# Whole-row query weights for layers 0 and 1, stored head columns for layers 2 and 3, and another order of steps at the layer ends

## The chip, the cores and the metric

The kernel runs on one core of one Trainium2 chip. The metric is the device time of one execution in microseconds (us). The kernel before took 2003.76 us (median of three runs, 2003.35 to 2005.01). A profiled execution gives a span (first to last instruction) shorter than the time of the same execution: 2002.9 us in the profile of before.

In the profiles PE is TensorE (matmuls; PEld are its weight loads), DVE is VectorE, ACT is ScalarE, POOL is GpSimd, and SP is SyncE, which issues the loads. The granted clock is the share of TensorE's full clock that the profile records at a time.

## The reference

Four attention layers decode one token. Layers 0 and 2 use the tensors A, layers 1 and 3 the tensors B. Each layer has its own pass over the whole cache:

```python
D, H, Sk, Dh = 640, 32, 8192, 192          # bfloat16
def _A_ref(x, k_cache, v_cache, wq, wo):   # _B_ref is the same
    q = (x @ wq).reshape(...)              # 1 x 32 heads x 192
    scores = einsum("bhqd,bhkd->bhqk", q, k_cache) * Dh ** -0.5
    p = softmax(scores)
    o = einsum("bhqk,bhkd->bhqd", p, v_cache)
    return o.reshape(...) @ wo
for l in range(4):                         # A, B, A, B
    x = x + ref(layernorm(x), ...)
```

K and V of one head are 3072 KB each; 32 heads, two tensors and four layers give most of the 849 MB that the profile counts. The query weights wq are 640 x 6144, 7680 KB.

## The kernel before

The kernel keeps eight slots in SBUF, of 128 x 12288 bfloat16, one K or V tile each. One queue issues all loads in the order of `plan`; a load waits until the tile that held its slot has been used. The engines work through `steps`: "m" (products: DVE multiplies K by q in place, in four pieces, and PE sums the products into S with 24 matmuls), "s" (softmax), "v" (values: 32 matmuls on PE), "wq" (query columns from a part of wq), "wc" and "wo" (output projection). The output weights of the last two heads, "wol", are a separate small load.

```python
HEADS_W, Q_FIRST, O_LAST, NSLOT = 10, 2, 2, 8
KEPT = {0: {("k", 0), ("v", 0)}, 1: {("v", 28), ("v", 29), ("v", 30), ("v", 31)}}
Q_PARTS = [(c, min(2, DC - c)) for c in range(0, DC, 2)]      # DC = 5: 2 + 2 + 1 chunks of rows
# ... cut ...
steps, plan = [], []
for l in range(NL):
    if l == 0:
        plan.append(("k", 0, 0))
        plan.append(("wq0", 0))
    wq_early = l == 2
    if wq_early:
        plan += [("wq", l, g) for g in range(len(Q_PARTS))]
    for p in range(H):
        if p > 0 and p % HEADS_W == 0:
            b = p // HEADS_W - 1
            steps.append(("wc", l, b))
            if p <= H - HEADS_W:
                plan.append(("wo", l, b))
                steps.append(("wo", l, b))
        if first_load("k", l, p) == ("k", l, p) and (l, p) != (0, 0):
            plan.append(("k", l, p))
        if stays("k", l, p):
            plan.append(("t", l, p))
        if wq_early and p == 0:
            part = [("wq", l, 0), ("m", l, 0), ("wq", l, 1), ("s", l, 0), ("v", l, 0), ("wq", l, 2)]
        elif p < H - 2:
            part = [("m", l, p), ("s", l, p), ("v", l, p)]
        elif p == H - 2:
            part = [("m", l, p)]
        else:
            part = [("m", l, p), ("s", l, p - 1), ("s", l, p), ("v", l, p - 1), ("v", l, p)]
        steps += part
        plan += [n for n in part if n[0] == "v" and first_load(*n) == n]
        if not wq_early:
            for g in {0: [0], 1: [1, 2]}.get(p, []):
                plan.append(("wq", l, g))
                steps.append(("wq", l, g))
        if p == H // 2 + 4 and l + 1 < NL:
            plan.append(("wq0", l + 1))
    plan.append(("wo", l, 2))
    steps.append(("wo", l, 2))
    plan.append(("wol", l))
at = {n: i for i, n in enumerate(steps)}

# ... cut ...
```

`KEPT` tiles stay in SBUF for the layer two further on: K and V of head 0 from layer 0 to layer 2, V of heads 28 to 31 from layer 1 to layer 3. So at the end of layer 1 six of the eight slots hold kept tiles and two rotate. The columns of wq for the first two heads, `wq0`, are a load of their own in every layer, because a layer can begin when these have landed:

```python
if n[0] == "wq0":
    return SP.op(lambda s: s.dma_start(
        wq0[:], w["wq"][:, o["q0"]:o["q0"] + Q_FIRST * DH].rearrange("(p c) n -> p c n", c=DC)),
        freed.get(("wq0", l - 1)), sem=semQ0, inc=16)
if n[0] == "wol":
    wol = slot[place[("wo", l, 2)]][:, NW * D:(NW + OI) * D].rearrange("p (i n) -> p i n", n=D)
    return SP.op(lambda s: s.dma_start(
        wol, w["wo"][o["wol"] * DH:(o["wol"] + O_LAST) * DH].rearrange("(p i) n -> p i n", p=P)),
        sem=semOL, inc=16)
```

The eviction of the value sums to SBUF, one instruction a head:

```python
ev_os[h] = last["O"][par] = last["rl"][par] = AC.op(
    lambda a: a.activation(o_sb[:], OB[par][:, 0:2 * DH], ACT.Copy, scale=rl[par][:, 0:1]),
    e, ev_rl[h], last["osb"], bank=use[f"O{par}"])

```

## Time and profile before

| | before |
|---|---|
| time, median of three | 2003.76 us |
| span of the profiled execution | 2002.9 us |
| PE, DVE, ACT busy | 70%, 52%, 11% |
| share of DMA in the chain of waits | 70% |
| a 3072 KB transfer lands every | 7.30 us |
| last K landing to final addition (the tail) | 25.8 us |

These are lines of the profile page of before. The first two rows have a digit or number for each of 40 equal slices of 50 us: the busy share of the DMA engines in tenths, and what they moved. The last is the chain of work that ended last.

```profile
DMA  9999999999999999999999999999999999999997
GB/s 404 433 430 426 431 430 426 431 431 428 425 431 429 431 429 430 426 432 428 429 375 432 430 429 431 431 427 430 429 429 428 430 428 431 431 429 429 429 431 321
...
DMA packets 44055, 850.65 MB, mean 425 GB/s; under 512 B 4800, under 2 KB 7360, under 8 KB 7872
...
HBM read 849.35 MB, written 0.00 MB: 424 GB/s over the span
...
DMA 70%; PE 17%; DVE 12%; ACT 1%; issue 1%; another core or an unknown queue 0%; SPq 0%; DVEq 0%
```

Nearly every slice is at about 430 GB/s, so the queue's time is the kernel's time. Three slices fall short: the start (404), the slice at 1000 to 1050 us (375) and the end (321). The slice at 1000 us holds the end of layer 1. Here is that end in the timeline of before. The columns are start, duration, engine, line, operation, out<-in, shapes, count, and in brackets the idle time before it and what ended it.

```profile
992.65 6.76 DVE L433 TENSOR_TENSOR slot<-slot,q_sb 128x3072 bf16<-128x3072 bf16 x4 [2.19 <-DMA slot<-in_B_k_cache_dram]
...
999.96 6.76 DVE L433 TENSOR_TENSOR slot<-slot,q_sb 128x3072 bf16<-128x3072 bf16 x4 [0.54 <-DMA slot<-in_B_k_cache_dram]
1006.64 0.68 DVE L453 TENSOR_REDUCE s_sb<-S 128x64 f32<-128x512 f32 x1
1006.77 1.46 PE L58 MATMUL S<-slot,ident 128*128 128x512 bf16 x6 [0.21 <-DVE slot L433]
...
1018.24 0.58 ACT L490 ACTIVATE o_sb<-O,small 128x384 f32<-128x384 f32 x1 [1.25 <-PE O L482]
...
1020.31 3.16 PE L402 MATMUL YB<-oT,slot 128*128 128x1 bf16 x75 [0.22 <-DMA slot<-in_B_wo_dram]
...
1024.10 0.38 SPq L272 DMA_DIRECT2D slot<-in_A_wq_dram  x1
1024.11 0.16 DVE L559 TENSOR_TENSOR small<-small,YB 128x5 f32<-128x5 f32 x1 [11.67 <-PE YB L402]
...
1038.75 0.34 SPq L269 DMA_DIRECT2D slot<-in_A_k_cache_dram  x1
```

**L** is the landing of head 30's K, the last but one of layer 1 (992.63 us in before, just ahead of the first line). The products of heads 30 and 31 follow each other at once, 7.3 us apart, as their K tiles land. **z** is the addition that closes the layer (1024.11, or L+31.5). At about the same time the queue, whose fastest part had nothing left from 1020.28 on (the slowest landed its last data at 1028.33), gets its next load, the second part of layer 2's wq. **Next K** is the first K that layer 2 loads; it is issued at 1038.75 (L+46.1) and lands at 1049.96 (L+57.3).

By the slowest of a transfer's 16 parts, next K landed 10.7 us after its predecessor instead of 7.3: this is the stall of 3.4 us that the prediction speaks of.

A landing here is always that of the slowest of a transfer's 16 parts. The Trainium skill, "DMA: Bandwidth & Descriptors", Why a DMA increments its semaphore by 16, says that only the full 16 means that all data landed. The landing records agree that it matters: the first and last part of head 30's K landed 8.1 us apart (984.52 and 992.63), and compute began 0.02 us after the last.

### The profile page before, as it was taken

The numbers are of one execution on the slowest core, as the hardware profiler recorded it, in microseconds if no ns is written. First come the engines' busy times: TensorE is split into PE (matmuls) and PEld (weight loads), VectorE is DVE, ScalarE is ACT, GpSimd is POOL, SyncE is SP. The second block draws the span as 40 slices with busy tenths as digits, with TensorE's granted clock in tenths as the row PEclk, the third lists the DMA queues.
The fourth block names the chain that finished last, engine by engine and source line by source line (L and its number), as shares of the span: only waits on it lengthen the run. The fifth ranks groups of instructions, "written<-read, shape, count | busy, mean of one in ns | idle before, by whom it ended". The sixth has DMA issues, their size and how long they took to land.

```text
span 2002.9 us, 20412 instructions
## 1 busy us (share of the span) xinstructions
PE 1406.5 (70%) x10438; PEld 323.9 (16%) x7494; DVE 1047.1 (52%) x1072; ACT 217.6 (11%) x657; POOL 4.6 (0%) x22
## 2 busy tenths in 40 slices
PE   5666767667667767767777676676677768767667
PEld 1111111111211111111131111111112212111112
DVE  3454554556345456455535546545564465554554
ACT  0111111111011111111101111111110111111110
POOL 0000000000000000000000000000000000000000
PEclk8788888888688798787878888888886888887887
DMA  9999999999999999999999999999999999999997
GB/s 404 433 430 426 431 430 426 431 431 428 425 431 429 431 429 430 426 432 428 429 375 432 430 429 431 431 427 430 429 429 428 430 428 431 431 429 429 429 431 321
DMA packets 44055, 850.65 MB, mean 425 GB/s; under 512 B 4800, under 2 KB 7360, under 8 KB 7872
## 3 DMA queue, kind: packets, MB, share of 16 engines
q1 hardware_dynamic: 43824, 849.37, 99.3%
q8 instruction: 70, 1.15, 0.2%
q14 instruction: 17, 0.14, 0.0%
q10 hardware_dynamic: 144, 0.00, 0.0%
HBM read 849.35 MB, written 0.00 MB: 424 GB/s over the span
## 4 chain that ended last, share of the span: by engine, by line
DMA 70%; PE 17%; DVE 12%; ACT 1%; issue 1%; another core or an unknown queue 0%; SPq 0%; DVEq 0%
DMA slot<-in_A_k_cache_dram 35%; DMA slot<-in_B_k_cache_dram 34%; PE S L58 11%; DVE slot L433 10%; PE O L482 2%; DMA slot<-in_A_wq_dram 1%; PE S L446 1%; PE TB L497 1%; DVE s_sb L453 1%; ACT p_sb L463 1%; PE TB L467 0%; PE QT L366 0%; DVE small L460 0%; PE YB L402 0%
## 5 line engine op out<-in xcount | busy, mean ns | idle before, releaser
L433 DVE TENSOR_TENSOR slot<-slot,q_sb 128x3072 bf16<-128x3072 bf16 x512 | 865.8, 1753 | 465.3 <-DMA slot<-in_A_k_cache_dram 239.5
L58 PE MATMUL S<-slot,ident 128*128 128x512 bf16 x2944 | 795.6, 424 | 34.1 <-DVE slot L433 34.1
L482 PE MATMUL O<-slot,p_sb 128*2 128x384 bf16 x4096 | 356.8, 428 | 0.0
L446 PE MATMUL S<-slot,ident 128*128 128x512 bf16 x128 | 60.9, 476 | 249.4 <-DVE slot L433 249.2
L453 DVE TENSOR_REDUCE s_sb<-S 128x64 f32<-128x512 f32 x128 | 88.4, 691 | 241.6 <-PE S L58 241.6
L482 PEld LDWEIGHTS O<-slot,p_sb 128*2 128x2 bf16 x4096 | 130.5, 88 | 138.9 <-issue 106.5
L497 PE MATMUL TB<-o_sb,small 128*1 128x192 f32 x480 | 124.0, 391 | 36.3 <-DVE small L471 28.0
L392 ACT ACTIVATE q_sb<-QM 128x192 bf16<-128x192 f32 x120 | 39.7, 331 | 970.7 <-PE QM L385 970.7
L385 PEld LDWEIGHTS QM<-ident,qT 128*128 128x128 bf16 x240 | 23.0, 98 | 731.2 <-issue 715.9
L467 PE MATMUL TB<-small,ones 128*128 128x1 f32 x256 | 50.7, 267 | 109.9 <-ACT p_sb L463 109.9
L457 PE MATMUL QM<-ident,m_bf 128*128 128x128 bf16 x128 | 27.7, 216 | 129.5 <-DVE m_bf L456 129.5
L490 ACT ACTIVATE o_sb<-O,small 128x384 f32<-128x384 f32 x128 | 74.4, 581 | 238.8 <-PE O L482 238.8
L471 DVE RECIPROCAL small<-TB 128x1 f32<-128x1 f32 x128 | 21.5, 168 | 123.3 <-PE TB L467 123.3
L463 ACT ACTIVATE p_sb<-s_sb,small 128x64 bf16<-128x64 f32 x128 | 44.5, 348 | 290.7 <-DVE small L460 290.7
L446 PEld LDWEIGHTS S<-slot,ident 128*128 128x128 bf16 x128 | 12.7, 99 | 331.3 <-DVE slot L433 330.9
L460 DVE TENSOR_REDUCE small<-QM 128x1 f32<-128x128 f32 x128 | 37.3, 291 | 53.2 <-PE QM L457 53.2
L467 PEld LDWEIGHTS TB<-small,ones 128*128 128x128 f32 x256 | 39.9, 196 | 129.6 <-ACT p_sb L463 129.6
L503 ACT ACTIVATE orow<-TB 1x192 bf16<-1x192 f32 x120 | 38.4, 320 | 205.4 <-PE TB L497 205.4
L497 PEld LDWEIGHTS TB<-o_sb,small 128*1 128x1 f32 x480 | 33.5, 89 | 77.7 <-DVE small L471 37.2
L457 PEld LDWEIGHTS QM<-ident,m_bf 128*128 128x128 bf16 x128 | 12.2, 96 | 208.1 <-ACT q_sb L392 131.6
L402 PE MATMUL YB<-oT,slot 128*128 128x1 bf16 x900 | 37.9, 178 | 3.1 <-ACT oT L417 2.2
L402 PEld LDWEIGHTS YB<-oT,slot 128*128 128x128 bf16 x900 | 36.9, 131 | 3.9 <-ACT oT L417 2.9
(47 smaller groups left out, 220.3 us busy)
## 6 DMA issues: line engine op xcount, KB each, us to landing
slot<-in_B_k_cache_dram SPq DMA_DIRECT2D x64, 3072.0 KB, 36.1
slot<-in_A_k_cache_dram SPq DMA_DIRECT2D x63, 3072.0 KB, 23.2
slot<-in_A_v_cache_dram SPq DMA_DIRECT2D x63, 3072.0 KB, 26.3
slot<-in_B_v_cache_dram SPq DMA_DIRECT2D x60, 3072.0 KB, 36.9
slot<-in_A_wo_dram SPq DMA_DIRECT2D x6, 2400.0 KB, 26.3
slot<-in_B_wo_dram SPq DMA_DIRECT2D x6, 2400.0 KB, 34.0
slot<-in_A_wq_dram SPq DMA_DIRECT2D x4, 2880.0 KB, 22.2
slot<-in_B_wq_dram SPq DMA_DIRECT2D x4, 2880.0 KB, 30.7
```

Source lines behind the costliest of these rows:

```text
L58: return t.add_instruction(mybir.InstMatmult(name=t.bass.get_next_instruction_name(), engine=mybir.EngineType.PE, ins=[t.lower_ap(rhs), t. ...
L392: lambda a: a.activation(q_sb[i][:], QM[:, 0:DH], ACT.Copy), e, last["q"][i], bank=use["QM"])
L402: e = PE.op(lambda t, i=i, c=c, f=y_first[0], fin=fin: t.matmul(YB[:, c:c + 1], lhsT=t3[:, i, c:D:DC], rhs=o[:, i:i + 1], start=f, stop=fi ...
L433: e = DV.op(lambda v, d0=d0: v.tensor_tensor(k3[:, :, d0:d0 + QD], kin[:, :, d0:d0 + QD], q_sb[qi][:, d0:d0 + QD].unsqueeze(1).broadcast_t ...
L446: t.matmul(S[:, :], lhsT=ident[:], rhs=k3[:, :, d0:d0 + R], start=True, stop=fin) if d0 == 0 else
L453: ev_s = DV.op(lambda v: v.tensor_reduce(s_sb[par][:], S[:].rearrange("p (j r) -> p j r", r=R), AX.X, ALU.add), ev_S[h], last["s"][par], b ...
L457: e = PE.op(lambda t: t.matmul(QM[:, C_MX:C_MX + P], lhsT=m_bf[par][:, 0:1].broadcast_to([P, P]), rhs=ident[:], start=True, stop=True), ev ...
L463: ev_p[h] = AC.op(lambda a: a.activation(p_sb[par][:], s_sb[par][:], ACT.Exp, bias=negm[par][:, 0:1], accum_out=l_col[par][:]), ev_n, ev_s ...
L467: e = PE.op(lambda t: t.matmul(TB[:, C_L + par:C_L + par + 1], lhsT=ones[:], rhs=l_col[par][:], start=True, stop=True), ev_p[h], last["L"] ...
L482: e = PE.op(lambda e, g=g, j=j, f=m < G, fin=fin: e.matmul(OB[par][32 * g:32 * g + 2, 0:2 * DH], lhsT=p_sb[par][:, j:j + 2], rhs=t[:, j * ...
L490: lambda a: a.activation(o_sb[:], OB[par][:, 0:2 * DH], ACT.Copy, scale=rl[par][:, 0:1]),
L497: e = PE.op(lambda t, i=i: t.matmul(TB[0:1, C_O:C_O + DH], lhsT=pick[:, i:i + 1], rhs=o_sb[:, i * DH:(i + 1) * DH], start=(i == 0), stop=( ...
```

## The change

The intent is to take small packets out of the queue and to shorten the chain at the layer ends.

1. Layers 0 and 1 load wq as one transfer of whole rows, 61,440 B each, over three neighbouring slots. The slots become one tensor `pool`.
2. While that wq is in SBUF, DVE copies the first two heads' columns for the layer two further on. Layers 2 and 3 load no `wq0`.
3. The last two heads of a layer get another order: the softmax of head 30 before the products of head 31, and its values before the softmax of head 31.
4. Other edits at layer ends: layers 2 and 3 take wq as 1 + 2 + 2 chunks instead of 2 + 2 + 1. The small output weights lie beside the next layer's wq part instead of beside the large ones, so the slot of the large ones is free after the first projection. The last layer's large output weights are split. The value sums of the last two heads are evicted in two pieces. Layer 3's first wq part comes before its first K, and the constant `ones` shrinks to one column that is broadcast.

```diff
+    Q_PARTS = [[(0, 2), (2, 2), (4, 1)] if l < 2 else [(0, 1), (1, 2), (3, 2)] for l in range(NL)]
+        pool = sb("pool", [P, NSLOT * TS], BF16)
+        slot = [pool[:, i * TS:(i + 1) * TS] for i in range(NSLOT)]
+        wq0 = [sb(f"wq0{i}", [P, DC, Q_FIRST * DH], BF16) for i in range(2)]
 ... cut ...
-                    part = [("m", l, p), ("s", l, p - 1), ("s", l, p), ("v", l, p - 1), ("v", l, p)]
+                    part = [("s", l, p - 1), ("m", l, p), ("v", l, p - 1), ("s", l, p), ("v", l, p)]
-                if p == H // 2 + 4 and l + 1 < NL:
-                    plan.append(("wq0", l + 1))
 ... cut: placement of three neighbouring slots, of the small output weights, the split of the last load ...
+            elif n[0] == "wq" and l < 2:
+                f = lambda s: s.dma_start(pool[:, i * TS:i * TS + DC * QW], w["wq"].rearrange("(p c) n -> p (c n)", c=DC))
 ... cut ...
+                q0 = ORDER[l + 2]["q0"]
+                ev_first[l] = DV.op(lambda v: v.tensor_copy(wq0[l][:], whole[:, :, q0:q0 + Q_FIRST * DH]), e)
 ... cut ...
-                ev_os[h] = last["O"][par] = last["rl"][par] = AC.op(
-                    lambda a: a.activation(o_sb[:], OB[par][:, 0:2 * DH], ACT.Copy, scale=rl[par][:, 0:1]),
+                if h < H - O_LAST:
+                    parts = [(o_sb[:], OB[par][:, 0:2 * DH])]
+                else:
+                    q = 1 if O_PART[l] == P else O_PART[l] // O_LAST // 8
+                    parts = [(o_sb[:, i * DH:(i + 1) * DH].rearrange("p (i e q) -> p q e i", i=OI[l], q=q),
+                              OB[par][:, i * DH:(i + 1) * DH].rearrange("p (q e i) -> p q e i", i=OI[l], q=q))
+                             for i in range(2)]
```

## The prediction

> **What bounds it now.** The DMA queue. The slices show DMA 9/10 busy and 425-433 GB/s, except the first (404), the one at 1000-1050 us (375, end of layer 1) and the last (321). The chain of waits is 70% DMA (K transfers). A 3072 KB transfer lands every 7.30 us; PE (70%) and DVE (52%) wait for data. So three things pay: queue time, queue stalls, and the tail after the last K.
>
> The landing records show each transfer's 16 parts spreading: first and last are 8.1 us apart at 1010 us, 2.0 after the stall there, 8.3 at the end. The slowest part releases compute; I count on it.
>
> **Queue time removed.** The four 480 KB loads of the first heads' columns cost 1.40-1.46 us each in landing spacing (2.1 in start-up): 2560 packets of 768 B, 36 ns each, while 19,200 B take 718 ns and 24,576 B 915 ns. The line through those two leaves 14 ns fixed per packet; the Trainium skill ("DMA: Bandwidth & Descriptors", Why small descriptors are slow) tells of a fixed cost per packet; this trace agrees. After: layers 2 and 3 load none (-1.46 us each). Layers 0 and 1 load 61,440 B rows: estimated 8 x 2.27 = 18.1 us against 40 x 0.435 + 1.46 = 18.9 now, -0.7 each. Splitting the last output-weight load: +0.06. Together -4.3 us, all on the critical path.
>
> **End of layer 1.** Six slots hold kept tiles, two rotate. Now the slowest part waits about 3.4 us (next K lands 10.7 us after its predecessor, not 7.3): the second wq part is issued at 1024.1, when both output projections are done, the first K of layer 2 at 1038.8, after 90 query matmuls (2.6 us) that delay its slot. After: the second wq part waits for the first projection only, and 45 matmuls come first. But softmax of head 30 (2.8 us of DVE in line) now precedes head 31's products, so the layer ends about 2 us later. Stall 3.4 -> 2.2: -1.2 us.
>
> **Other boundaries.** Layer 1's whole wq needs three free slots, but some 20 us of V and wo are queued behind the last K when they come free (8-12 us after landing): no stall. First products move from 17.0 to about 28 us; initial transfers last to about 50, slots are free by about 35: no cost. The column copy (1-2 us DVE) is off the path.
>
> **Tail.** From the last K landing (1973.9) to the final add (1999.7) the chain is DVE/PE, not DMA (last weights land 1995.4). Products 31 start about 3.1 us later; against that, values 30 no longer stand behind softmax 31 (-2.9). Output projection: 90 matmuls before and after. Net 0, +-1.
>
> **Prediction.** 2003.8 - 4.3 - 1.2 = 1998.2 us, range 1993.5 to 2001.5. Faster by over 2%: 0.01; within: 0.98; slower: 0.01.
>
> **What would show it.** HBM read 848.37 MB, no 768 B packets; whole wq landing about 18 us after its predecessor; slice at 1000-1050 at 380-395 GB/s; first K of layer 2 landing about 3 us earlier; softmax between products 30 and 31 on DVE; last slice about unchanged.
>
> **What would make it wrong.** 61,440 B rows moving at another rate; a DMA gap at layer 0/1; the slowest part drifting otherwise (its lag grows in steps near 0.6-1.3 us, probably instruction fetches of 16 KB): +-1.5; another PE clock in the tail (0.5 now); the layer-1 gap closing fully (-2) or growing.

## More of the kernel before

The Trainium skill, "Perfetto Trace Analysis", Optimization Strategy, says that a kernel sometimes has several regimes, with a most-contended engine that changes over time. This trace agrees: the queue, at about 430 GB/s, sets the time in nearly all slices, and the chain from L to next K in this one (375 GB/s).

The windows view of before shows the same place in stretches of 5 us. Its columns are the stretch, its length, the busy time and count of PE, PEld, DVE, ACT and POOL, then the granted TensorE clock, the DMA share and GB/s.

```profile
1000.00:1005.00 5.00, 4.89 (x22) 0.10 (x1) 5.00 (x4) 0.00 (x0) 0.00 (x0) 1.00 0.97 413
1005.00:1010.00 5.00, 3.32 (x15) 0.40 (x3) 3.21 (x7) 0.44 (x2) 0.00 (x0) 1.00 1.01 434
...
1020.00:1025.00 5.00, 4.26 (x93) 4.09 (x93) 0.43 (x5) 0.17 (x1) 0.00 (x0) 0.74 0.62 259
...
1035.00:1040.00 5.00, 5.00 (x73) 1.54 (x59) 0.91 (x2) 0.00 (x0) 0.00 (x0) 0.89 0.79 280
```

PE is busy and at full clock while the last scores are summed, and the queue falls to 259 GB/s only from 1020 us on. It is short again from 1035 to 1040 us (280 GB/s), until next K is issued.

## The result, and the profile after

The changed kernel took 2004.01 us (median of four runs, 2001.93 to 2005.47); before took 2003.55 us in its four runs. Ratios here are from the runs of both kernels in the same rounds, so they are not quite the ratio of the quoted medians or means. The ratio is 1.0002, with a 95% interval from 0.9984 to 1.0019. The predicted gain of 5.5 us did not come. The spans of the two profiled executions differ by 1.3 us (2001.53 against 2002.86), which lies inside the interval.

Lines of the page of after:

```profile
DMA  9999999999999999999989999999999999999997
GB/s 412 430 430 431 430 429 428 432 430 430 429 428 431 430 429 430 430 430 430 429 351 431 430 429 429 431 431 429 429 430 427 428 430 430 431 429 431 428 431 319
...
DMA packets 40487, 849.67 MB, mean 425 GB/s; under 512 B 4688, under 2 KB 4688, under 8 KB 5328
...
HBM read 848.36 MB, written 0.00 MB: 424 GB/s over the span
...
DMA 66%; PE 20%; DVE 11%; ACT 1%; issue 1%; another core or an unknown queue 0%; SPq 0%; DVEq 0%
```

The 2560 packets of 768 B and 0.99 MB are gone, as intended. But the slice at 1000 us fell from 375 to 351 GB/s, where 380 to 395 was predicted, and DMA's share of the chain fell from 70% to 66% in favour of PE. Here is the same place in the timeline of after:

```profile
989.84 6.76 DVE L492 TENSOR_TENSOR pool<-pool,q_sb 128x3072 bf16<-128x3072 bf16 x4 [1.97 <-DMA pool<-in_B_k_cache_dram]
...
999.90 0.69 DVE L512 TENSOR_REDUCE s_sb<-S 128x64 f32<-128x512 f32 x1 [3.30 <-PE S L58]
...
1002.56 6.75 DVE L492 TENSOR_TENSOR pool<-pool,q_sb 128x3072 bf16<-128x3072 bf16 x4
1004.76 7.63 PE L58 MATMUL S<-pool,ident 128*128 128x512 bf16 x23
...
1019.12 0.94 ACT L556 ACTIVATE o_sb<-O,small 128x192 f32<-128x192 f32 x2 [2.38 <-PE O L541]
...
1021.49 3.16 PE L462 MATMUL YB<-oT,pool 128*128 128x1 bf16 x75
...
1024.68 0.38 SPq L324 DMA_DIRECT2D pool<-in_A_wq_dram  x1
...
1025.28 0.16 DVE L630 TENSOR_TENSOR small<-small,YB 128x5 f32<-128x5 f32 x1 [9.66 <-PE YB L462]
...
1037.68 0.34 SPq L319 DMA_DIRECT2D pool<-in_A_k_cache_dram  x1
```

L is 989.82, so all that came before it gained 2.8 us. Then DVE, which had been done with head 30's products at 996.60, stood idle for 3.30 us until PE had summed their scores. Only then came the softmax, and only after it head 31's products: at L+12.7, where before had them at L+7.3. z came at L+35.5 instead of L+31.5, and next K landed at 1049.58, L+59.8 instead of L+57.3. Of the 2.8 us, 2.4 had been given back.

The windows of after, in the same columns as above:

```profile
1000.00:1005.00 5.00, 1.23 (x5) 0.50 (x4) 3.63 (x6) 0.44 (x2) 0.00 (x0) 0.80 1.00 427
1005.00:1010.00 5.00, 5.00 (x13) 0.00 (x0) 4.31 (x3) 0.00 (x0) 0.00 (x0) 0.52 0.94 403
1015.00:1020.00 5.00, 3.78 (x46) 2.03 (x46) 0.17 (x1) 1.05 (x3) 0.00 (x0) 0.66 0.81 336
1020.00:1025.00 5.00, 4.88 (x100) 4.87 (x101) 0.00 (x0) 0.23 (x2) 0.00 (x0) 0.50 0.06 22
...
1035.00:1040.00 5.00, 4.96 (x104) 2.42 (x91) 1.83 (x4) 0.00 (x0) 0.00 (x0) 1.00 1.03 436
```

PE had little to do from 1000 to 1005 us (1.23 us of 5, before 4.89), because it waited for products that waited for the softmax. In the next stretch its clock was 0.52, and 13 score matmuls filled 5.00 us, where before did 12 and three small ones in 3.32 us at clock 1.00. The queue moved almost nothing (22 GB/s) from 1020 to 1025 us. The stall had changed its place. By the slowest of a transfer's 16 parts, the second wq load landed 12.8 us after the first (7.1 in before, for 6.9 us of data), next K only 7.6 us after its predecessor. The first wq load is 1440 KB here instead of 2880 KB, so the queue had less to do while the layer ended.

The part from L to next K in pieces, from the two traces (us; each figure is rounded by itself):

| piece | before | after | difference |
|---|---|---|---|
| L to start of head 31's products | 7.3 | 12.7 | +5.4 |
| to end of head 31's score matmuls | 8.3 | 9.8 | +1.6 |
| to z | 15.9 | 12.9 | -3.0 |
| z to issue of next K | 14.6 | 12.4 | -2.2 |
| issue to landing of next K | 11.2 | 11.9 | +0.7 |
| sum, L to next K | 57.3 | 59.8 | +2.4 |

From next K to the last K of layer 3 after gained another 1.6 us, mostly the wq0 of layer 3 that is not loaded (1.40 us in before). The last K landed at 1971.95 against 1973.90. The tail from there to the final addition was 26.0 us against 25.8.

### The profile page after: what moved, and what is told of

It reads as the page before. It is cut to its first block, busy times and chain, and to the rows that moved or that the text cites. A ratio compares the mean times of both kernels' runs of the same rounds, so it can differ in the third digit from the quotient of the medians. Undisturbed runs are those within 1.5% of the kernel's fastest.

```text
span 2001.5 us, 20412 instructions
## 1 busy us (share of the span) xinstructions
PE 1399.3 (70%) x10438; PEld 321.3 (16%) x7494; DVE 1049.4 (52%) x1074; ACT 219.8 (11%) x665; POOL 4.5 (0%) x22
## 4 chain that ended last, share of the span: by engine, by line
DMA 66%; PE 20%; DVE 11%; ACT 1%; issue 1%; another core or an unknown queue 0%; SPq 0%; DVEq 0%
DMA pool<-in_A_k_cache_dram 32%; DMA pool<-in_B_k_cache_dram 31%; PE S L58 13%; DVE pool L492 10%; PE O L541 2%; DMA pool<-in_B_wq_dram 1%; DMA x_bf<-in_A_x_dram 1%; PE TB L564 1%; PE S L505 1%; DVE s_sb L512 1%; PE QT L424 1%; PE YB L462 1%; ACT p_sb L522 1%; PE TB L526 0%
## 5 line engine op out<-in xcount | busy, mean ns | idle before, releaser
L492 DVE TENSOR_TENSOR pool<-pool,q_sb 128x3072 bf16<-128x3072 bf16 x512 | 865.6, 1753 | 431.5 <-DMA pool<-in_A_k_cache_dram 221.5
L58 PE MATMUL S<-pool,ident 128*128 128x512 bf16 x2944 | 795.5, 424 | 35.8 <-DVE pool L492 35.7
L541 PE MATMUL O<-pool,p_sb 128*2 128x384 bf16 x4096 | 354.0, 426 | 0.0
L505 PE MATMUL S<-pool,ident 128*128 128x512 bf16 x128 | 60.1, 469 | 231.3 <-DVE pool L492 231.3
L541 PEld LDWEIGHTS O<-pool,p_sb 128*2 128x2 bf16 x4096 | 130.0, 88 | 169.5 <-issue 137.0
L556 ACT ACTIVATE o_sb<-O,small 128x384 f32<-128x384 f32 (+1 forms) x136 | 77.3, 580 | 273.9 <-PE O L541 273.9
L505 PEld LDWEIGHTS S<-pool,ident 128*128 128x128 bf16 x128 | 12.7, 99 | 289.9 <-DVE pool L492 289.8
L462 PE MATMUL YB<-oT,pool 128*128 128x1 bf16 x900 | 38.0, 178 | 2.2 <-ACT oT L476 2.2
L462 PEld LDWEIGHTS YB<-oT,pool 128*128 128x128 bf16 x900 | 37.0, 131 | 2.9 <-ACT oT L476 2.9
## 6 DMA issues: line engine op xcount, KB each, us to landing
pool<-in_B_k_cache_dram SPq DMA_DIRECT2D x64, 3072.0 KB, 35.5
pool<-in_A_wo_dram SPq DMA_DIRECT2D x6, 2400.0 KB, 26.8
```

What stands on the lines that cost most here:

```text
L58: return t.add_instruction(mybir.InstMatmult(name=t.bass.get_next_instruction_name(), engine=mybir.EngineType.PE, ins=[t.lower_ap(rhs), t. ...
L462: e = PE.op(lambda t, i=i, c=c, f=y_first[0], fin=end and i == k - 1: t.matmul(YB[:, c:c + 1], lhsT=t3[:, i, c:D:DC], rhs=o[:, i:i + 1], s ...
L492: e = DV.op(lambda v, d0=d0: v.tensor_tensor(k3[:, :, d0:d0 + QD], kin[:, :, d0:d0 + QD], q_sb[qi][:, d0:d0 + QD].unsqueeze(1).broadcast_t ...
L505: t.matmul(S[:, :], lhsT=ident[:], rhs=k3[:, :, d0:d0 + R], start=True, stop=fin) if d0 == 0 else
L541: e = PE.op(lambda e, g=g, j=j, f=m < G, fin=fin: e.matmul(OB[par][32 * g:32 * g + 2, 0:2 * DH], lhsT=p_sb[par][:, j:j + 2], rhs=t[:, j * ...
L556: ev_os[h] = AC.op(lambda a, o=o, i=i: a.activation(o, i, ACT.Copy, scale=rl[par][:, 0:1]), e, ev_rl[h], last["osb"], bank=use[f"O{par}"])
```

## The experiments

The first theory (T1) was that the order of the last two heads costs what the queue gained. The rivals were that the queue's gain is smaller than estimated, that the two-piece eviction or the placement of the small weights costs it, and that the restart of the queue after layer 1 is decided by when the second wq part is issued and not by the compute chain. All kernels gave correct results. They ran in four sets, each with its own nine runs of before. Times are medians of five runs; times of one set differ by chip from another's, so ratios are what to compare.

### The order alone, in both kernels

`a_oldorder` is after with one line put back; `b_neworder` is before with that line put in.

```diff
 (a_oldorder; b_neworder has the reverse edit in the kernel before)
-                    part = [("s", l, p - 1), ("m", l, p), ("v", l, p - 1), ("s", l, p), ("v", l, p)]
+                    part = [("m", l, p), ("s", l, p - 1), ("s", l, p), ("v", l, p - 1), ("v", l, p)]
```

> The changed kernel with one thing undone: at layer ends the order of the last two heads is that of before (products 31, then softmax 30, softmax 31, values 30, values 31). I call T the landing (slowest part) of the last K of layer 1. Measured from T to the landing of the next K loaded (second head of layer 2): 50.0 us before, 52.4 after. Theory (order): the new order makes layer 1 end about 4 us later (T+24.2 before, T+28.1 after), the second wq part waits for that layer's output projection, so the queue runs dry. With the old order the layer ends near T+24, the second wq part is issued near T+23.4, and T to next K is 47 to 48 us, so the kernel is 4 to 5 us shorter than the changed one, near 1998 us, 5 to 6 us below before. Rival (the smaller first wq part, 1440 instead of 2880 KB, leaves too little in the queue, and the order costs nothing): T to next K stays 51 us or more and the time within 1.5 us of the changed kernel.

> The kernel before with one thing done: the new order of the last two heads alone. Theory (order costs): layer 1 ends near T+28, T to next K grows from 50.0 to about 53 us, the tail stays within 1 us, so the kernel is about 3 us slower than before (2006 to 2007 us). Rival (order costs nothing, the queue part sizes do): T to next K stays within 0.7 us of 50.0, and the time equals that of before within 1 us.

Measured: a_oldorder 2000.93 us, ratio 0.9985 [0.9973, 0.9998]; b_neworder 2006.13 us, ratio 1.0008 [0.9995, 1.0020]. With the old order head 31's scores ended at L+15.6 again, and with the new order in the kernel before at L+21.1. Both times moved in the direction of T1, but neither is clear of noise by itself: b_neworder's interval holds 1, and a_oldorder's overlaps after's. a_oldorder's time missed the expected 1998 us, and the marks that the expectations named missed too. From the last K of layer 1 to next K it took 51.7 us in a_oldorder (47 to 48 expected, the rival's mark was 51 or more) and 50.0 us in b_neworder (about 53 expected, the rival's mark was 50.0). In b_neworder that last K itself landed 1.7 us late (L+9.0), and from L, which later expectations use, next K moved from L+57.3 to L+59.0. In a_oldorder z was still at L+33.9 (before L+31.5) and next K at L+59.0, hardly earlier than in after. So the order isn't the only cost at the end of layer 1: in this trace both sets of value matmuls ran at half clock (2.73 us each; 2.73 and 1.47 in before), and the two-piece eviction was still there.

### Filling the queue earlier

`c_wo_early` is after with layer 1's large output weights ahead of the last V, and projected before the last values. That frees their slot, and so the second wq part of layer 2, earlier. `d_wo_early_tail` does the same at the last layer too.

```diff
+EARLY = (1,)                        # d_wo_early_tail: (1, 3)
 ... cut ...
+                if l in EARLY and p == H - 1:
+                    part = part[:-1] + [("wo", l, 2)] + part[-1:]
                 steps += part
-                plan += [n for n in part if n[0] == "v" and first_load(*n) == n]
+                plan += [n for n in part if n[0] == "wo" or n[0] == "v" and first_load(*n) == n]
 ... cut: no second "wo" after the last head; the last values are gathered before the small projection ...
```

> The changed kernel with the last large output weight of layer 1 loaded ahead of the last V instead of behind it, and multiplied ahead of the last values, so that its slot is free for the second wq part about 8 us sooner; the new order stays. Theory (the gap is made by the second wq part waiting for the layer's end): the second wq part is issued near T+17 instead of T+27.5, no gap in the queue before it, T to next K 46.5 to 48 us, about 5 us less than the changed kernel, about 1998 us. Rival (the gap is bandwidth or start-up of transfers after the layer end, whatever the issue): T to next K stays above 50.5 us.

> The one before it in this list, with the same done at the end of layer 3: there the first 12 columns of the last large output weight come ahead of the last V and are multiplied ahead of the last values, the 3 other columns while ScalarE evicts the last values, and the small output part last. Boundary as in the one before. Tail: from the landing of the last K of layer 3 to the final addition 26.0 us in the changed kernel (25.8 before); expected 24.7 us, so 1.3 us less in all, about 1996.5 us. If the tail was bound by the last V's landing instead, it would grow by about 3 us, since that V now lands 4.6 us later.

Measured: c_wo_early 2004.23 us, ratio 0.9997 [0.9984, 1.0009]; d_wo_early_tail 2002.89 us, ratio 0.9997 [0.9983, 1.0010]. The second wq part was issued at L+28.4 instead of L+34.9, with hardly a gap for the slowest part before it (it landed 7.3 us after the first), and still next K landed at L+59.1, against L+59.8 in after. The gap had only moved: the third part was issued at L+39.1, and next K's slot comes free with head 0's products, which stand behind z (L+34.5), so next K was issued at L+48.2. In after itself the loads behind the second part landed one right after another, so there its issue did set the landing of next K; but the gate that stands behind it is less than 1 us away. This is against the rival, and against the prediction, which had booked a gain for an earlier second part. The expected times (about 1998 and 1996.5 us) were both missed. The tail of d_wo_early_tail (24.9 us) is no shorter than that of c_wo_early (24.6), whose tail is unchanged; no gain is shown there.

`e_k_slot` attacks the new gate: c_wo_early, with the query columns of the second wq part computed before head 0's products, so that next K can take that part's slot.

```diff
-                steps.append(("wq", l, 0))
+                steps += [("wq", l, 0), ("wq", l, 1)]
-                    part = [("m", l, 0), ("wq", l, 1), ("s", l, 0), ("v", l, 0), ("wq", l, 2)]
+                    part = [("m", l, 0), ("s", l, 0), ("v", l, 0), ("wq", l, 2)]
```

> The kernel with the output weight ahead of the last V of layer 1, plus one thing: the second wq part's query columns run on PE ahead of head 0's product matmuls, so that the next K takes that wq part's slot and not the slot of head 0's K. Theory (what gates the restart is the slot that head 0's products free, at the end of a DVE/PE chain from L, not the wq parts): the next K is issued at about L+42.5 instead of L+48.2 and lands at L+55.5 to L+57, against L+59.1 in the kernel without this; 2 to 3 us less in time than that kernel. Rival (the restart is gated by wq parts or by bandwidth): next K still lands at L+58.5 or later.

Measured: 2002.91 us, ratio 0.9991 [0.9979, 1.0004]. Next K was issued at L+43.0, five us earlier, and landed at L+58.9 all the same, which is what its rival had forecast. In the plan it stands behind the third wq part, which was issued only at L+40.6 and landed at L+50.2, because its slot waits for the first part's query columns, behind z. Its tail was 26.8 us, with the same code there as c_wo_early (24.6): the tail alone varies by 2 us from trace to trace.

### The parts of the change

`g_wq_only` keeps points 1 and 2 of the change and undoes 3 and 4. `f_one_evict` is after with the one-piece eviction.

```diff
 (g_wq_only against after, core)
-    Q_PARTS = [[(0, 2), (2, 2), (4, 1)] if l < 2 else [(0, 1), (1, 2), (3, 2)] for l in range(NL)]
+    Q_PARTS = [[(0, 2), (2, 2), (4, 1)] for l in range(NL)]
-                    part = [("s", l, p - 1), ("m", l, p), ("v", l, p - 1), ("s", l, p), ("v", l, p)]
+                    part = [("m", l, p), ("s", l, p - 1), ("s", l, p), ("v", l, p - 1), ("v", l, p)]
-            if n[0] == "wol" and n[1] + 1 < NL:  ...
+            if n[0] == "wol":
                 before[n] = []               # the small output weights lie beside the large ones
 (both, against after)
-                for o, i in parts:
-                    ev_os[h] = AC.op(lambda a, o=o, i=i: a.activation(o, i, ACT.Copy, scale=rl[par][:, 0:1]),
+                ev_os[h] = AC.op(lambda a: a.activation(o_sb[:], OB[par][:, 0:2 * DH], ACT.Copy, scale=rl[par][:, 0:1]),
```

> The first part of the change alone: whole rows of wq in layers 0 and 1, the first heads' columns copied for layers 2 and 3; everything at layer ends as before (order of the last two heads, one-piece eviction, small output part behind the large one in its slot, two-column first wq parts, no split at the end). I call L the landing of the next-to-last K of layer 1. Before: next K of layer 2 is issued at L+46.1 and lands at L+57.3; the changed kernel L+47.9 and L+59.8. Theory (whole rows gain what was predicted, the layer-end edits of the change lose it at the end of layer 1): L is about 2.8 us earlier than in before, the next K lands at L+57 to L+57.8, the last K of layer 3 lands 4 to 4.5 us earlier than before, and the kernel is 3.5 to 4.5 us faster than before, 2 us or more faster than the changed kernel. Rival (the saved queue time itself does not survive the end of layer 1, whatever the order there): next K at L+59 or later, gain at most 2 us.

> The changed kernel with the last two heads' results evicted in one piece of 384 (as before, 0.58 us) instead of two strided pieces (0.94 us together), the gather reading with a stride again. If the two pieces are part of what makes layers end later, layer 1 ends 0.7 us sooner than in the changed kernel (L+34.8 instead of L+35.5), and the tail is 0.7 us shorter; if they are hidden, nothing moves. In time at most 1.5 us below the changed kernel, not clear of noise.

Measured: g_wq_only 2000.17 us (1999.31 to 2000.71), ratio 0.9978 [0.9965, 0.9992]; f_one_evict 2002.95 us, ratio 0.9995 [0.9983, 1.0008]. g_wq_only is 4.4 us faster than before (means 2000.10 and 2004.48), and its last K landed at 1969.23 us, 4.67 earlier than before's: the predicted queue time was there. In f_one_evict z was at L+34.9, as expected if the eviction counts, but next K at L+60.0: the eviction alone doesn't explain the end of layer 1.

The page's GB/s row of g_wq_only:

```profile
GB/s 411 429 431 430 428 430 431 430 429 429 431 428 430 431 429 429 430 431 429 430 383 430 428 431 431 429 430 429 430 430 427 430 429 430 431 428 431 430 431 314
```

The slice at 1000 us is at 383, inside the 380 to 395 that had been predicted for after. The timeline of g_wq_only there:

```profile
997.21 6.76 DVE L484 TENSOR_TENSOR pool<-pool,q_sb 128x3072 bf16<-128x3072 bf16 x4 [0.54 <-DMA pool<-in_B_k_cache_dram]
1003.89 0.69 DVE L504 TENSOR_REDUCE s_sb<-S 128x64 f32<-128x512 f32 x1
...
1021.43 0.16 DVE L612 TENSOR_TENSOR small<-small,YB 128x5 f32<-128x5 f32 x1 [11.44 <-PE YB L451]
...
1035.20 0.34 SPq L308 DMA_DIRECT2D pool<-in_A_k_cache_dram  x1
```

Head 31's products start at L+7.3 with a wait of 0.54 us for their K, not for a softmax, and next K is issued at 1035.20, landing at 1046.76 (L+56.9; 2.8 us earlier than after). Its windows show the clock:

```profile
1000.00:1005.00 5.00, 5.00 (x25) 0.10 (x1) 4.80 (x5) 0.00 (x0) 0.00 (x0) 1.00 1.00 428
1005.00:1010.00 5.00, 2.00 (x18) 0.98 (x18) 1.73 (x6) 0.88 (x4) 0.00 (x0) 1.00 0.99 423
```

### After again

The unchanged kernel after, in the same set as e, f and g, to see how far two traces of one kernel differ.

> The changed kernel unaltered, to compare in the same rounds and to have a second trace: next K of layer 2 lands at L+59.8 within 1 us, layer 1 ends at L+35.5 within 1 us, and the time is within 1.5 us of before. If the clock granted to PE at the end of layer 1 varies from run to run, the layer's end moves by up to 1.3 us per set of 32 value matmuls (1.5 or 2.7 us each).

Measured: 2003.63 us, ratio 0.9998 [0.9985, 1.0010]. z was at L+34.6 (below f_one_evict's, without its edit) and next K at L+58.8, about 1 us less than in the first trace, so +1.5 us against before instead of +2.4. A difference of 1 us between two traces' marks is therefore not evidence by itself.

### The remaining parts, one at a time

`i_parts` is a_oldorder with the one-piece eviction: g_wq_only plus the placement edits. `g_neworder` is g_wq_only with the order line of after. `h_wo_early_old` is i_parts with the early output weights of c_wo_early. `j_order_l1` is g_wq_only with the order at layer 1 only.

```diff
 (i_parts against a_oldorder: the eviction edit shown above)
 (g_neworder against g_wq_only)
-                    part = [("m", l, p), ("s", l, p - 1), ("s", l, p), ("v", l, p - 1), ("v", l, p)]
+                    part = [("s", l, p - 1), ("m", l, p), ("v", l, p - 1), ("s", l, p), ("v", l, p)]
 (h_wo_early_old against i_parts: the EARLY edit shown above)
 (j_order_l1 against g_wq_only)
+                    if l == 1:
+                        part = [("s", l, p - 1), ("m", l, p), ("v", l, p - 1), ("s", l, p), ("v", l, p)]
```

> The whole-row kernel (wq alone, which was 4.4 us faster than before) plus the edits of where transfers go: small output part beside a one-column first wq part, other wq order in layer 3, last large weight in two transfers. Old order and one-piece eviction stay. With z the first addition after layer 1 and L the landing of the next-to-last K of that layer: in the whole-row kernel z is at L+31.55 and the next K lands at L+56.9. Theory (only the new order and the two-piece eviction make the layer end late; the other edits gain when it ends early): z within 1 us of L+31.5, next K issued near L+44.5, landing at L+55 to L+56.5; time equal to the whole-row kernel or 1 to 2 us faster (1998 to 2000). Rival (the smaller first wq part costs too): next K at L+57.5 or later, time 1 us or more above the whole-row kernel.

> The whole-row kernel plus the new order of the last two heads alone. Theory (the order loses the gain): head 31's score matmuls end near L+21.5 instead of L+15.9, z moves from L+31.55 to L+33.5 to L+35.5, the next K lands at L+58.5 to L+60 instead of L+56.9, and the time rises by 2 to 3 us to about 2002 to 2003. Rival (the order is neutral): z within 0.7 us of L+31.55 and time within 1 us of the whole-row kernel.

> The kernel of the first run in this list, plus the large output weight ahead of the last V of layer 1: the candidate for the fastest. z then waits for the last V (landing L+27.6): L+32 to L+33, second wq part issued near L+27 instead of L+31, next K issued near L+44.5 to 45.5 (still the slot that head 0's products free) and landing at L+55 to L+56.5; time within 1 us of the first in this list, 1998 to 1999.5, and below both before and the changed kernel.

> The whole-row kernel plus the new order of the last two heads at the end of layer 1 only; the other three layer ends keep the old order. With the new order at all four ends it rose by about 2.8 us, of which the traces put about 0.9 us in the tail. Theory (the cost sits at the end of layer 1 and in the tail): layer 1's closing addition moves from L+31.55 to L+33.5 to L+35.5, the next K is issued 1 us or more later, the tail is as in the whole-row kernel (last K landing to final addition 25.8, within 0.7), and the time is 1 to 2.5 us above the whole-row kernel, 2001 to 2002.5 us. Rival (the cost comes from the ends of layers 0 and 2 or from the tail alone): time within 0.7 us of the whole-row kernel.

Measured:

| kernel | time, us | ratio [95%] | scores of 31 end | z | next K lands | tail |
|---|---|---|---|---|---|---|
| i_parts | 2000.95 | 0.9979 [0.9967, 0.9992] | L+15.6 | L+33.1 | L+57.3 | 25.8 |
| g_neworder | 2002.93 | 0.9992 [0.9979, 1.0004] | L+21.3 | L+34.1 | L+57.5 | 26.7 |
| h_wo_early_old | 2001.15 | 0.9981 [0.9967, 0.9995] | L+15.6 | L+33.8 | L+57.7 | 25.8 |
| j_order_l1 | 2001.73 | 0.9987 [0.9974, 1.0001] | L+19.8 | L+31.7 | L+57.5 | 25.4 |

- i_parts is equal to g_wq_only in time, so the placement edits bring nothing that shows and cost nothing that shows. Its z (L+33.1) and next K (L+57.3) missed the expectation: both sets of value matmuls ran at half clock, 2.73 us for 32, and in g_wq_only both took 1.47 us.
- g_neworder gave 2.8 us back against g_wq_only by the ratios of two sets (0.9992 - 0.9978 = 0.0014 of 2004 us), whose intervals overlap. Within its own set it is clear: its five runs (2002.30 to 2003.84) all lie above the ten of i_parts and h_wo_early_old, which have the old order (at most 2001.90). Its next K moved by only 0.6 us, less than expected; its tail is 0.9 longer.
- h_wo_early_old shows that earlier output weights give nothing with the old order either; next K is still gated by the slot of head 0's products. Its expected time, z and next K were all missed.
- j_order_l1 missed its expectation of z: L+31.7, no later than g_wq_only. In this trace the clock came back to full at L+16.3 and PE stayed at full clock through both sets of values, and the projection had to wait for its weights to land anyway. So what the order costs at layer 1 depends on the granted clock; this run neither shows nor excludes a cost in time (1.8 us more than g_wq_only by the ratios, 1.6 in median, with intervals that overlap).

### All runs together

The twelve timed results that hold the whole-row wq, sorted by the order of the last two heads:

| order | kernels and ratios | mean of (mean this - mean before) |
|---|---|---|
| old everywhere | g 0.9978, i 0.9979, h 0.9981, a 0.9985 | -3.6 us |
| new at layer 1 only | j 0.9987 | -2.7 us |
| new everywhere | e 0.9991, g_neworder 0.9992, f 0.9995, c 0.9997, d 0.9997, after_again 0.9998, after 1.0002 | -0.9 us |

Single intervals overlap (each is about 2.6 us to either side), but the groups don't mix: all four kernels with the old order are faster than all seven with the new one. The order costs some 2.8 us on average here. The groups also differ in the eviction; with one piece alone (g, i, h against f and g_neworder) the difference is 2.7 us, with two pieces alone (a against the other five) it is 2.0 us. The traces, one of each kernel, show about half of it: the spans of the seven are on average 1.5 us longer than those of the four, 1.2 of it between L and next K. Where the rest arises is not shown.

The reason for the part at layer 1 is visible in all nine traces with the new order there. DVE waited 1.55 to 3.30 us for head 30's scores before that softmax (3.30 in after, 2.39 in after_again, 2.00 in g_neworder, 1.55 in j_order_l1), and head 31's products started 3.7 to 5.4 us later than L+7.3. Between the scores of heads 30 and 31 PE had only small matmuls for 4.5 us, and in all nine the clock record fell to half between L+11.4 and L+13.2, after that pause, for 6.8 us (3.4 in d_wo_early_tail and j_order_l1), just when head 31's scores are summed. In the five traces with the old order (before, a_oldorder, g_wq_only, i_parts, h_wo_early_old) the clock was full from L+7.6 at the latest until L+18.2 or later. The windows of b_neworder, the kernel before with that one line, show it too (L is 992.83):

```profile
1000.00:1005.00 5.00, 2.18 (x11) 0.39 (x3) 2.00 (x5) 0.44 (x2) 0.00 (x0) 0.93 0.98 418
1005.00:1010.00 5.00, 3.91 (x10) 0.10 (x1) 5.00 (x4) 0.00 (x0) 0.00 (x0) 0.50 1.02 435
```

Before had 1.00 in both stretches. The Trainium skill, "TensorE: Matmul & The Clock Gate", What's actually happening, says that the throttled clock is the default, that activity releases it, and that it is judged in free-running windows of about 3.4 us. These traces agree: the records change in steps of 3.4 us, 32 value matmuls take 1.47 us at full and 2.73 us at half clock, and the place of the steps shifts from trace to trace. That PE's pause causes the drop is inferred from its place in all nine traces; no run held the clock and changed the pause alone.

## Why the prediction was right or wrong

- **What bounds the kernel: right.** Queue time taken away came off the time in g_wq_only.
- **Queue time, -4.3 us: right.** g_wq_only measured -4.4 us in time and -4.67 at the last K, -0.46 of which arose at the end of layer 1. The fastest of the 16 parts of layer 1's whole wq landed 18.1 to 18.2 us after that of its predecessor in four traces (18.1 estimated; by the slowest part it was 18.1 in g_wq_only and 19.5 in after), and a packet of 61,440 B took 2.267 us in the median (2.27 estimated). In after the gain is in the trace too: 2.8 us at L, 1.6 us after next K. The estimate used a fixed 14 ns per packet, worked out from two packet sizes; the Trainium skill, "DMA: Bandwidth & Descriptors", Why small descriptors are slow, names a fixed overhead per packet as one of two reasons. The largest size lies on that line; the 768 B packets, at 36 ns, lie some 6 ns below it.
- **Tail, 0 +- 1: right for after** (26.0 and 25.8 against 25.8), though with the order alone it was 0.9 longer in two pairs of traces (before to b_neworder, g_wq_only to g_neworder); that is within the 2 us by which the tail varies.
- **End of layer 1, -1.2 us: wrong, and the step that failed.** The prediction put it so: "softmax of head 30 (2.8 us of DVE in line) now precedes head 31's products, so the layer ends about 2 us later. Stall 3.4 -> 2.2". Measured from L to next K it was +2.4 us in the first trace of after and +1.5 in the second, 2.7 to 3.6 us off. Three things are in it:
  1. The wait was left out: the softmax's 2.8 us of DVE were counted, but not the wait of DVE for the scores that the softmax reads. The softmax took 2.7 us and the wait 3.3; less the 0.54 us that before had waited for its K, head 31's products started 5.4 us later in after.
  2. The scores of head 31 then ran at half clock, +1.6 us. The prediction named another clock as a danger for the tail only. Of these 7.0 us, 3.0 came back, much as the predicted -2.9. So the layer ended 4.0 us later (3.1 in after_again), not 2.
  3. The stall was forecast to shrink from 3.4 to 2.2 us at next K. There it nearly vanished (7.6 us after its predecessor, for 7.3 of data), but 6.0 us of stall came up ahead of the second wq part, which is issued only when the late layer has done its large projection. The gain from an earlier second part was booked as if its issue alone decided when next K lands: c_wo_early issued it 6.5 us earlier and next K still landed at L+59.1. What counts is the chain from L through z to head 0's products, and e_k_slot shows another gate beside it. That 45 query matmuls instead of 90 stand before head 0's scores is not shown to help: from z to issue of next K g_neworder, with 90, took 12.5 us and a_oldorder, with 45, took 14.0. Of the 2.2 us gained there in after, more than half lies in head 0's score matmuls themselves (6.7 us against 7.9); the clock came back to full 2.7 us after their start, in before 5.3.
- **The total.** 2003.8 - 4.3 - 1.2 became, in the traces, -2.8 to L, +2.4 to next K, -1.6 to the last K, +0.2 in the tail: -1.8 at the final addition, and -1.3 in the span, as the store of the result took some 0.4 us longer. The medians differ by +0.5 us instead, 1.8 more. Nearly all of that is which executions were profiled: before's took 2004.88 us, 1.3 above the median of its four runs, and after's 2003.68 us, 0.3 below. So the pair of traces makes after look better than its runs do. The range, 1993.5 to 2001.5, did not hold 2004.01; within 2% was right.

Left open is the exact split among the order, the two-piece eviction (0.94 us instead of 0.58 for one head) and the granted clock. From a_oldorder to i_parts taking the two pieces away brought 1.2 us of time, and from after to f_one_evict about 0.6, both inside the intervals; next K in a_oldorder was at L+59.0 and in i_parts at L+57.3, but in after and f_one_evict it was no different. Which of these a given run pays depends on where the clock steps fall.

The fastest kernel is g_wq_only, the whole-row load and the stored columns alone: 0.9978 of before, and faster than after in the same set (2000.10 against 2003.86 us). It is still within 2% of both.

## What to carry to other kernels

Where a queue is the bound, take out its small packets and cost it by packet size; that estimate held to a few tenths of a microsecond. When an order of steps is changed, don't only add the moved work to the engine it moves to: ask what that work waits for. Here DVE stood idle for another engine's result (3.30 us in after), and the engine that starved in the meantime came back at half clock. A gap in a queue is worth closing only if nothing after it waits for something else, so follow the chain to the load that must land, and test each edit of a bundle by itself: here one half of a change paid 4.4 us and the other half gave most of it back. Look, too, at where a profiled execution lies among the runs before traces of two kernels are subtracted.

## What the Trainium skill lacked or had wrong

- "DMA: Bandwidth & Descriptors" doesn't tell that the 16 parts of transfers on one queue drift apart over a long kernel: first and last were 8.1 us apart at the end of layer 1, 2.0 after the stall there, and 8.3 at the end. In before the lag grew mostly in nine jumps of 0.6 to 1.5 us, each in a transfer during or just before which one of the run's 70 instruction fetches fell (16,384 B, about 1.07 us a packet); that they cause it is inferred.
- The same page's table of bandwidth by size, measured on transfers that GpSimd issues, ends at 425 GB/s for 16 MB; it has no row for transfers queued back to back from SyncE. Such transfers of 3072 KB, each landing 7.30 us after the one before, ran at 431 GB/s here.
- The same page gives about 600 ns to the first byte for loads that SyncE issues, and a cost of start and completion together only for those that GpSimd issues. Here, in after, a 2880 KB load issued when the queue had run dry took 8.79 us from issue to the landing of its fastest part, for 6.9 us of data: 1.9 us for start and completion together.
- No page has the time of packets as large as 61,440 B; it was 2.267 us in the median, against 0.915 us for 24,576 B and 0.718 us for 19,200 B.
- "TensorE: Matmul & The Clock Gate" explains the drop of the clock after a pause and shows it on a matmul loop that waits for DMA. It has no case like this one, where the order of steps on another engine makes the pause: 24 score matmuls ended 9.8 us after the start of their products instead of 8.3.
